# An S4 convolution beside a gated linear unit: the first normalisation moved to ScalarE, lag 2048 brought in by accumulating DMAs, the last tile split 384 and 128, and a new order

## The chip, the cores and the metric

The kernel runs on 1 core of one Trainium2 chip. The metric is the device time of one execution in microseconds (us), the median of several runs. The core has five engines, and each works through its own queue of instructions in order: TensorE (PE in the profile; its weight loads are PEld), VectorE (DVE), ScalarE (ACT), GpSimd (POOL) and SyncE (SP), which here issues nearly all DMAs.

## The reference

A layer normalisation without weights feeds two branches, whose outputs are added to the input. L = 2048 tokens, D = 512 channels, N = 128 modes a channel, F = 1792; inputs and output are bf16.

```python
x  = A_u                                   # (1, 2048, 512)
xn = (x - mean(x)) / sqrt(var(x) + 1e-5)   # over the 512 channels

# branch A: a long convolution in every channel
dt = exp(log_dt)
K  = real(sum_n C[d,n] * exp(dt*A[d,n])**l * dt*B[d,n])   # (512, 2048)
y  = irfft(rfft(pad(xn.T, 2L)) * rfft(pad(K, 2L)))[:, :L] # cast to bf16
yA = y.T + xn * Dskip

# branch B: a gated linear unit
h  = sigmoid(xn @ w_gate) * (xn @ w_up)    # (2048, 1792)
yB = h @ w_down

out = x + yA + yB
```

## The kernel before

**Start.** The 2048 tokens are 16 tiles of 128. Statistics are taken on VectorE (L542, L543; tile 2's on ScalarE instead, L533 to L538). From the variance comes 1/sqrt(var + eps): for the first four tiles VectorE adds epsilon (L486) and copies the mean (L489), POOL takes the square root as a power (L492), VectorE the reciprocal (L493); for the other groups of four tiles POOL adds epsilon (L481) and takes the power (L482). L554 normalises on VectorE. The first four tiles are transposed on TensorE (L565) and evicted into `xnT`, a pair of tiles at a time: the first pair whole by ScalarE (L572), the second whole by VectorE (L574). The others go through DRAM. While the inputs load, TensorE runs fillers (`keep_warm`, L519: 12, and then 3, 1 and 1).

**Branch B.** Four groups of 512 tokens, in each 14 tiles of F: gate (L1045), up (L1069), sigmoid on ScalarE (L1057), the product on VectorE (L1089, or L1094 straight from PSUM), then down (L1123). Its matmuls fill TensorE between those of branch A.

**Branch A.** The powers exp(dt A)^l are made as a table by squaring (L792 to L798) and complex products on VectorE (L737, L738, L742, L743). From the table TensorE makes pieces of K (L823). They are evicted to `kq_sb` (L288 on ScalarE, L286 on VectorE, by the list `ON_DVE`), stored to `k_scr` in DRAM and loaded again as `kT`, and L845 adds Dskip to lag 0. The convolution is a transform of xn (L695, then through `z_scr` in DRAM, L885), copies that swap halves (`f_sw`, L898), a transform of K (L911), the product of the two spectra on VectorE (L916, L920), an inverse transform in eight groups (L935), and a second step (S2, L994), for which the groups go through `v_scr` in DRAM.

**Lag 2048.** The transforms leave out one term for a few tokens. `f_rz` (L952) works out eight small values for each channel, L964 transposes them, ScalarE evicts them into `rr`, and S2 adds them with matmuls against a table `sr` (L997) in the tiles 12 to 15.

**End.** S2 of twelve tiles is added to branch B by VectorE, two tiles at once (L1020; the rows of x are already in `glu_sb`, put there by accumulating DMAs of POOL, L1160). In the last four tiles S2 is accumulated on top of the down projection in PSUM, and VectorE adds the rows `xt` of x (L1143). The very last tile is made in two halves of 256 columns.

**Order.** Every piece of work is an operation with a number, its place in the list `pl.ops`. A written list, `ORDER`, gives the order in which they are issued to the engines' queues; nothing is decided at run time but waits on semaphores. `ON_DVE` holds the numbers of the evictions and normalisations that go to VectorE rather than ScalarE. The results of matmuls stand in PSUM, in two pairs of 128x1024 f32 (`pair_63`, `pair_64`) and four banks of 128x512 f32.

## Time and profile before

| What | Value |
| --- | --- |
| Runs, median of 3 | 213.82 us (213.72, 213.82, 217.08) |
| Span of the profiled execution | 213.6 us |
| Own time of the profiled execution | not given; its span is 0.2 us below the median of the runs |
| TensorE busy | 204.2 us (96%), 1838 matmuls |
| VectorE busy | 191.3 us (90%), 406 instructions |
| ScalarE busy | 177.1 us (83%), 284 |
| POOL busy | 27.8 us (13%), 32 |
| Moved by DMA | 42.61 MB, 199 GB/s over the span |

Busy time is the sum over the engine's instructions. The span runs from the first to the last instruction of the profiled execution, and times in it are counted from its start. The granted clock of TensorE is at full speed in all of the 40 slices of the page.

### The profile page before, as it was taken

The numbers are of one execution on the slowest core, as the hardware profiler recorded it, in microseconds if no ns is written. First come the engines' busy times: TensorE is split into PE (matmuls) and PEld (weight loads), VectorE is DVE, ScalarE is ACT, GpSimd is POOL, SyncE is SP. The second block draws the span as 40 slices with busy tenths as digits, with TensorE's granted clock in tenths as the row PEclk, the third lists the DMA queues.
The fourth block names the chain that finished last, engine by engine and source line by source line (L and its number), as shares of the span: only waits on it lengthen the run. The fifth ranks groups of instructions, "written<-read, shape, count | busy, mean of one in ns | idle before, by whom it ended". The sixth has DMA issues, their size and how long they took to land.

```text
span 213.6 us, 4875 instructions
## 1 busy us (share of the span) xinstructions
PE 204.2 (96%) x1838; PEld 102.9 (48%) x1864; DVE 191.3 (90%) x406; ACT 177.1 (83%) x284; POOL 27.8 (13%) x32
## 2 busy tenths in 40 slices
...
GB/s 148 316 383 381 100 147 324 61 98 147 110 126 104 76 105 229 213 191 151 249 185 141 228 202 237 215 221 175 202 188 208 217 284 274 141 357 218 240 213 172
DMA packets 52377, 42.61 MB, mean 199 GB/s; under 512 B 16641, under 2 KB 44546, under 8 KB 52354
## 3 DMA queue, kind: packets, MB, share of 16 engines
...
q10 hardware_dynamic: 832, 0.43, 0.8%
q8 instruction: 14, 0.23, 0.5%
...
## 4 chain that ended last, share of the span: by engine, by line
PE 41%; DVE 40%; POOL 6%; DMA 4%; issue 4%; ACT 3%; DVEq 0%; SPq 0%; ACTq 0%
PE pair L911 8%; PE bank L1045 7%; PE bank L1123 7%; PE bank L1069 7%; DVE big L737 6%; DVE big L738 6%; POOL ln_ve_b L481 5%; PE pair L935 5%; DVE big L742 4%; DVE big L743 4%; DVE stats L542 3%; DVE hT_sb L1094 3%; DVE hT_sb L1089 3%; DVE big L678 2%; DMA big<-v_scr 2%
## 5 line engine op out<-in xcount | busy, mean ns | idle before, releaser
L288 ACT ACTIVATE big<-pair 128x1024 bf16<-128x1024 f32 x64 | 64.5, 1039 | 6.9 <-DVE big L920 1.7
L1069 PE MATMUL bank<-xnT,wu_sb 128*128 128x512 bf16 x214 | 52.9, 379 | 1.7 <-issue 0.6
L1123 PE MATMUL bank<-wd_sb,hT_sb 128*128 128x512 bf16 (+1 forms) x231 | 50.6, 367 | 0.5 <-issue 0.2
L1045 PE MATMUL bank<-xnT,wg_sb 128*128 128x512 bf16 (+1 forms) x191 | 45.6, 370 | 1.0 <-issue 0.5
L1045 PEld LDWEIGHTS <-wg_sb 128*128 128x128 bf16 x240 | 22.5, 98 | 25.0 <-issue 3.2
L1123 PEld LDWEIGHTS <-hT_sb 128*128 128x128 bf16 x238 | 22.4, 98 | 24.9 <-issue 1.6
L1069 PEld LDWEIGHTS <-wu_sb 128*128 128x128 bf16 x224 | 20.7, 98 | 27.5 <-issue 5.4
L1057 ACT ACTIVATE hT_sb<-bank 128x512 bf16<-128x512 f32 x48 | 28.2, 627 | 0.7 <-PE bank L1045 0.7
L737 DVE TENSOR_TENSOR big<-big 128x1024 bf16<-128x1024 bf16 (+4 forms) x40 | 26.7, 667 | 0.2
L738 DVE TENSOR_TENSOR big<-big 128x1024 bf16<-128x1024 bf16 (+4 forms) x40 | 26.5, 663 | 0.0
L1084 ACT ACTIVATE us_sb<-bank 128x512 bf16<-128x512 f32 x40 | 23.6, 616 | 0.6 <-DVE hT_sb L1089 0.3
L911 PE MATMUL pair<-big 128*128 128x256 bf16 x160 | 19.8, 273 | 0.0
L916 DVE TENSOR_TENSOR big<-big 128x2048 bf16<-128x2048 bf16 x16 | 19.3, 1217 | 0.1
L911 PEld LDWEIGHTS <-big 128*128 128x128 bf16 x160 | 15.4, 98 | 4.7 <-issue 0.8
L481 POOL TENSOR_SCALAR ln_ve_b<-mvb 128x4 bf16<-128x4 bf16 x3 | 13.0, 4323 | 34.1 <-DVE mvb L543 34.1
L742 DVE TENSOR_TENSOR big<-big 128x512 bf16<-128x512 bf16 (+4 forms) x40 | 16.5, 413 | 0.2
L743 DVE TENSOR_TENSOR big<-big 128x512 bf16<-128x512 bf16 (+4 forms) x40 | 16.5, 412 | 0.0
L792 ACT ACTIVATE sq_sb<-big 128x256 bf16<-128x256 bf16 (+2 forms) x20 | 13.2, 658 | 1.6 <-DVE big L743 1.5
L1089 DVE TENSOR_TENSOR hT_sb<-hT_sb,us_sb 128x1024 bf16<-128x1024 bf16 x20 | 13.5, 683 | 0.0
L935 PE MATMUL pair<-big 64*64 64x512 bf16 (+1 forms) x256 | 13.1, 327 | 0.0
L898 DVE COPY big<-big 32x1024 bf16<-32x1024 bf16 x20 | 8.4, 418 | 4.5 <-ACT big L288 4.2
L288 ACT ACTIVATE big<-big 128x256 bf16<-128x256 bf16 x30 | 12.4, 452 | 0.0
...
## 6 DMA issues: line engine op xcount, KB each, us to landing
...
z_scr<-big SPq DMA_DIRECT2D x16, 256.0 KB, 2.9
big<-z_scr SPq DMA_DIRECT2D x16, 256.0 KB, 4.2
v_scr<-big SPq DMA_DIRECT2D x16, 256.0 KB, 3.2
...
```

Of the source, the lines that this page charges most:

```text
L288: nc.scalar.activation(out=get(out), in_=get(in_), func=ACT.Identity)
L481: P.tensor_scalar(out=q["ve_b"], in0=mvb[:, s, 1], scalar1=EPS, scalar2=None, op0=ALU.add)
L737: V.tensor_tensor(out=wide(outp), in0=wide(lo), in1=mre, op=ALU.mult)
L738: V.tensor_tensor(out=wide(tb()), in0=wide(lo), in1=mim, op=ALU.mult)
L742: V.tensor_tensor(out=outp[:, :, 0], in0=outp[:, :, 0], in1=tb()[:, :, 1], op=opr)
L743: V.tensor_tensor(out=outp[:, :, 1], in0=outp[:, :, 1], in1=tb()[:, :, 0], op=opi)
L911: T.matmul(two(sk)[:, o:o + DW], es()[:, g, kt, :], kTv[p][:, :, kt, :], start=kt in (0, NKT - 1), stop=kt >= NKT - 2)
L935: T.matmul(two(sv)[o:o + 64, DW * (2 * g + y):2 * DW * (g + 1)], mab[b:b + 64, 2 * u + g, q, :], pq()[b:b + 64, q, ch] if y else pp()[b:b ...
L1045: T.matmul(bank(sl, k % 2)[:, c0:c1], w[:, kt, k * 128:(k + 1) * 128], xnT[:, grp, kt, c0:c1], start=(kt == 0), stop=(kt == KT - 1))
L1057: S.activation(out=hT_sb[:, hs.idx, k % 2, :], in_=bank(sl), func=ACT.Sigmoid)
L1069: T.matmul(bank(sl), wu_sb[:, kt, k * 128:(k + 1) * 128], xnT[:, grp, kt, :], start=(kt == 0), stop=(kt == KT - 1))
L1123: T.matmul(bank(po)[:, 0:c[1] - c[0]], hT_sb[:, hts[k // 2].idx, k % 2, jj * 128:(jj + 1) * 128], wd_sb[:, k, c[0]:c[1]], start=first and ...
```

## The change

1. The first four tiles: the statistics go to `mv` in f32, and the power is replaced by two ScalarE instructions, a logarithm and an exponential, exp(-0.5 ln(var + eps)), with an explicit load of the ScalarE function table that holds both. Tile 2's statistics return to VectorE. In the other groups epsilon is added on ScalarE instead of POOL.
2. The evictions of the transposed first tiles are halved: four of 128x512, three on VectorE and one on ScalarE. The gate matmuls that use halves wait for these.
3. The fillers on TensorE: 9 ahead, and 3 after the first transposes.
4. Lag 2048: one transposing matmul with 32 rows, one eviction, one store to DRAM (`r_scr`), and two accumulating POOL DMAs that add the rows to `xt`. The table `sr`, the clearing of `rr` and the five matmuls L997 are gone.
5. The last tile is made in 384 and 128 columns. The 384 columns take S2 after the down projection, the 128 ahead of it, as both halves did before.
6. `ORDER` is new, and `ON_DVE` holds five operations more: an eviction of the first transform (128x1024), two small casts in the making of K's seeds (128x256), one eviction of `kq_sb` (128x768) and one of the second transform (128x2x2x256).

The core of the diff (the table `ORDER`, of 927 numbers before and 923 after, is left out):

```diff
-ON_DVE = (86, 89, 104, 106, 121, 122, 123, 137, 138, 184, 194, 195, 198, 199, 201,)
+ON_DVE = (81, 84, 99, 101, 116, 117, 118, 132, 133, 154, 179, 189, 192, 194, 226, 242, 289, 335, 361, 516,)
...
-    rz = const.tile([128, KT, 8], BF, name="rz")
+    rz = const.tile([128, 8, KT], BF, name="rz")
+    rr = const.tile([8 * KT, 128], BF, name="rr")
...
         if t1 <= LN_ACT:
-            o_v = pl.add("DVE", 0.17 + 0.53 * len(set(range(t0, t1)) & set(ON_ACT)), fv_, deps, prio)
-            o_w = pl.add("DVE", 0.14, fw_, [o_v], prio)
-            o_p = pl.add("POOL", 0.7, lambda: P.tensor_tensor(out=q["sd_b"], in0=q["ve_b"], in1=half[:, s], op=ALU.pow), [o_v], prio)
-            return pl.add("DVE", 0.15, lambda: V.reciprocal(out=q["ri_f"], in_=q["sd_b"]), [o_p, o_w], prio)
+            def fr_():
+                S.activation(out=lnv[:, s], in_=mv[:, s, 1], func=ACT.Ln, bias=epst[:])
+                S.activation(out=q["ri_f"], in_=lnv[:, s], func=ACT.Exp, scale=-0.5)
+            return pl.add("ACT", 0.45, fr_, deps, prio)
 
         def fm_():
+            S.activation(out=q["ve_b"], in_=mvb[:, s, 1], func=ACT.Identity, bias=epst[:])
             S.activation(out=q["m_f"], in_=mvb[:, s, 0], func=ACT.Identity)
...
+    S.add_instruction(mybir.InstLoadActFuncSet(name=nc.get_next_instruction_name(), act_func_set_id=LN_EXP_SET))
...
-    keep_warm(12, -10)
-    for n in (0, 5, 6):
-        keep_warm(3 if n < 3 else 1, -9 + n)
+    warm = [keep_warm(9, -10)]
...
+            tr = pl.add("PE", 0.80, ft, [xn_ready[i - 1], xn_ready[i], l_id] + warm[-1:], prio, acq=[sl])
+            if i == 1:
+                warm.append(keep_warm(3, prio, [tr]))
+            half_ready.append([])
+            for n, eng in enumerate(("DVE", "DVE" if i == 1 else "ACT")):
+                def fe(i=i, sl=sl, n=n, eng=eng):
+                    ks = slice(2 * n, 2 * n + 2)
+                    dst, src = xnT[:, 0, ks, (i - 1) * 128:(i + 1) * 128], bankb(sl).rearrange("p (k n) -> p k n", k=KT)[:, ks]
...
-    o_rt = pl.add("PE", 0.32, f_rt, [o_rz], 60, acq=[slr])
-    o_rz = pl.add("ACT", 0.48, lambda slr=slr: S.activation(out=rr[0:8, :], in_=bank(slr)[0:8, :], func=ACT.Identity), [o_rt, l_sr, m_rr], 60, rel=[slr])
+    o_rt = pl.add("PE", 0.08, lambda slr=slr: T.matmul(bank(slr)[0:8 * KT, 0:128], rz[:].rearrange("p q k -> p (q k)"), ident[:], start=True, stop=True),
+                  [o_rz], 60, acq=[slr])
+    o_rr = pl.add("ACT", 0.25, lambda slr=slr: S.activation(out=rr[:], in_=bank(slr)[0:8 * KT, 0:128], func=ACT.Identity), [o_rt], 60, rel=[slr])
+    r_st = dma("SP", r_scr[:], rr[:], deps=[o_rr], prio=60, pkt=256)(8 * KB)
...
-        if i >= 12:
-            T.matmul(o[64:128, :], sr[:, i - 12, :], rr[:, w[0]:w[1]], start=False, tile_position=(0, 64), **kw)
...
+                    def fc(n, xt=xt):
+                        with nc.allow_non_contiguous_dma(reason="laid out"):
+                            P.dma_start(out=xt[95:128:32, n::2, :], in_=r_v[n], accum_op=ALU.add)
+                    lx = [pl.add("POOL", 1.0, lambda n=n: fc(n), lx + [r_st], 3, dma=(4 * KB, _rate(256), 1.0)) for n in range(2)]
...
-            cols = [(0, 256), (256, 512)] if last else [(0, 512)]
-            ver = vp_op[i // 2] + [l_s2, o_rz]
+            cols = [(0, 384), (384, 512)] if last else [(0, 512)]
+            ver = vp_op[i // 2] + [l_s2]
```

What the new order does shows in the engines' queues. A row names a line and an operation, what it writes and reads and the shape; x2 stands for two in a row. Lines count in the kernel before and in the changed kernel: L565 becomes L548, L1045 L1031, L695 L684, L743 L732, L823 L812, L845 L834, L898 L885, L916 and L920 L903 and L907, L935 L922, L994 L981, L1020 L1006, L1094 L1080, L1123 L1115, L1143 L1136, L286 and L288 L285 and L287.

**VectorE at the start of the program**, before; `xnT` does not appear, since its first eviction is ScalarE's:

```order
L542 BN_STATS stats<-big 128x6 x2
L543 BN_AGGR mvb<-stats 128x2 x2
L486 TENSOR_SCALAR ln_ve_b<-mvb 128x2
L489 CAST ln_m_f<-mvb 128x2
L542 BN_STATS stats<-big 128x6
L543 BN_AGGR mvb<-stats 128x2
L493 RECIPROCAL ln_ri_f<-ln_sd_b 128x2
L554 TENSOR_SCALAR big<-big,ln_m_f,ln_ri_f 128x512 x2
L486 TENSOR_SCALAR ln_ve_b<-mvb 128x2
L489 CAST ln_m_f<-mvb 128x2
L493 RECIPROCAL ln_ri_f<-ln_sd_b 128x2
L554 TENSOR_SCALAR big<-big,ln_m_f,ln_ri_f 128x512 x2
```

And the same place now, behind the first two tiles' statistics (L599, L607 and L608 belong to the products with dt, and 128x2x256 are half evictions):

```order
L525 BN_STATS stats<-big 128x6
L526 BN_AGGR mv<-stats 128x2
L537 TENSOR_SCALAR big<-big,mv,ln_ri_f 128x512 x2
L525 BN_STATS stats<-big 128x6
L526 BN_AGGR mv<-stats 128x2
L562 COPY xnT<-pair_63 128x2x256
L537 TENSOR_SCALAR big<-big,mv,ln_ri_f 128x512 x2
L599 TENSOR_TENSOR big<-big 128x512 x2
L562 COPY xnT<-pair_64 128x2x256
L562 COPY xnT<-pair_63 128x2x256
L607 TENSOR_SCALAR big<-big 128x512
```

The third tile's statistics now stand ahead of the first normalisation, the small steps for epsilon, mean and reciprocal are gone, and the second half of the first pair (`pair_63`) comes behind the second pair's normalisation, two products with dt and the second pair's first half.

**VectorE at the second Dskip addition** (`dskr`), just behind the last complex products, before:

```order
L920 TENSOR_TENSOR big<-big 128x1024 x2
L898 COPY big<-big 32x1024 x4
L845 TENSOR_TENSOR big<-big,dskr 1x16x16
L898 COPY big<-big 32x1024 x4
L1094 TENSOR_TENSOR hT_sb<-hT_sb,bank_68 128x512
L916 TENSOR_TENSOR big<-big 128x2048
```

And now (the casts L285 are the evictions of `kq_sb` and of the second transform that were ScalarE's):

```order
L285 CAST kq_sb<-pair_63 128x96x8
L903 TENSOR_TENSOR big<-big 128x2048
L907 TENSOR_TENSOR big<-big 128x1024 x2
L1080 TENSOR_TENSOR hT_sb<-hT_sb,bank_67 128x512
L285 CAST big<-pair_64 128x2x2x256
L1080 TENSOR_TENSOR hT_sb<-hT_sb,bank_65 128x512
L834 TENSOR_TENSOR big<-big,dskr 1x16x16
L1080 TENSOR_TENSOR hT_sb<-hT_sb,bank_66 128x512
L885 COPY big<-big 32x1024 x8
L903 TENSOR_TENSOR big<-big 128x2048
```

The addition of Dskip stood behind four of the swapping copies; now it stands ahead of all eight, with three products of branch B and two evictions around it.

**SyncE near the end**, now, where the last groups of the inverse transform are stored and loaded again (`v_scr`) and the first output leaves:

```order
L422 DMA v_scr_103<-big 128x4x256 x2
L422 DMA xnT<-v_scr_102 128x2x1024
L422 DMA v_scr_104<-big 128x4x256
L422 DMA big<-v_scr_103 96x2x1024
L422 DMA r_scr<-rr 32x128
L422 DMA big<-v_scr_104 32x2x1024
L422 DMA big<-v_scr_103 96x2x1024 x2
L422 DMA big<-v_scr_104 32x2x1024
L422 DMA out_dram<-big 128x1024
L422 DMA big<-v_scr_103 96x2x1024
```

Before, two stores `v_scr_101` stood side by side here and both led to the reloads; now there is one, the store of the lag rows `r_scr` stands among the reloads, and one reload of `v_scr_103` has moved behind the first output.

97 lines of the change are left out of this document (39 added, 58 removed), and 81 rows, old and new, of the table ORDER.

## The prediction

> **What bounds the kernel now.** I read the page first: its span, the engines' shares (first section) and the shares of the chain that ended last (fourth section). Then, by windows, two stages of 20 us: their ends, then length, then busy time of PE, PEld, DVE and ACT.
>
> ```profile
> span 213.6 us, 4875 instructions
> PE 204.2 (96%) x1838; PEld 102.9 (48%) x1864; DVE 191.3 (90%) x406; ACT 177.1 (83%) x284; POOL 27.8 (13%) x32
> ...
> PE 41%; DVE 40%; POOL 6%; DMA 4%; issue 4%; ACT 3%; DVEq 0%; SPq 0%; ACTq 0%
> ...
> 120.00:140.00 20.00, 19.79 (x273) 10.60 (x275) 19.97 (x47) 19.02 (x30) 0.00 (x0) 1.00 0.76 211
> ...
> 160.00:180.00 20.00, 19.48 (x193) 10.95 (x192) 15.60 (x28) 18.50 (x24) 0.00 (x0) 1.00 0.83 240
> ```
>
> TensorE and VectorE share the chain almost evenly, and from 120 to 140 both are full; VectorE has room in 160 to 180 (15.60 of 20). So work taken from TensorE counts only if VectorE keeps up. The timeline (start, length, engine, line, operation, how many; in brackets the wait ahead and who ended it) shows that the program falls into pieces at three points: the last product that makes K (C, L823), the last inverse product (V, L935), and the first matmul of the last transform (S2, L994).
>
> ```profile
> 154.65 0.43 DVE L743 TENSOR_TENSOR big<-big 128x512 bf16<-128x512 bf16 x1
> ...
> 155.04 1.51 PE L823 MATMUL pair<-big 128*32 128x82 bf16 x128
> ...
> 163.95 1.71 DVE L898 COPY big<-big 32x1024 bf16<-32x1024 bf16 x4 [4.20 <-ACT big L288]
> 165.69 0.28 DVE L845 TENSOR_TENSOR big<-big,dskr 1x256 bf16<-1x256 bf16 x1
> ...
> 166.05 2.35 PE L911 MATMUL pair<-big 128*128 128x256 bf16 x20
> ...
> 188.06 1.28 DVE L920 TENSOR_TENSOR big<-big 128x1024 bf16<-128x1024 bf16 x2
> 188.35 1.51 PE L935 MATMUL pair<-big 64*64 64x512 bf16 x32
> ```
>
> C begins when VectorE ends its last complex product (L743) and ends at 156.55. From there to the end of V at 189.86 is 33.3 us. VectorE waits 4.20 us once and then has no idle time to 189.34. The chain in order of time goes on from there (start, length, who), and after it the timeline of VectorE:
>
> ```profile
> 190.22 1.03 ACT big L288
> 191.27 2.59 DMA v_scr<-big
> 193.92 4.70 DMA big<-v_scr
> 198.67 0.95 PE pair L994 x14
> ...
> 203.34 1.94 DVE L1143 TENSOR_TENSOR big<-bank,big 128x512 bf16<-128x512 f32 x3 [1.76 <-PE bank L997]
> ...
> 210.06 0.41 DVE L1143 TENSOR_TENSOR big<-bank,big 128x256 bf16<-128x256 f32 x1
> ```
>
> From V to S2 the way is an eviction, a store and a reload: 198.67 - 189.86 = 8.8 us. The last 10 us are VectorE's: from 203.34 to 210.47 its additions stand end to end, 14.9 us from S2 to the end of the span.
>
> The three runs are 213.72, 213.82 and 217.08; the span is 213.6, and no time of its own is given for the profiled execution. I add the terms to the span and then 0.2 for the way to the median.
>
> **Term 1, up to C.** The start first, from the timeline, and the group of ScalarE's smallest steps (busy, mean ns).
>
> ```profile
> 1.43 5.30 PE L519 MATMUL bank<-glu_sb 128*128 128x512 bf16 x12 [1.43 <-POOL rz L513]
> 7.10 1.24 PE L519 MATMUL bank<-glu_sb 128*128 128x512 bf16 x5
> 8.48 0.44 PEld L1045 LDWEIGHTS <-wg_sb 128*128 128x128 bf16 x4 [0.64 <-DMA wg_sb<-in_B_w_gate_dram]
> 8.61 0.60 PE L1045 MATMUL bank<-xnT,wg_sb 128*128 128x256 bf16 x4 [0.26 <-ACT xnT L572]
> 11.57 0.60 PE L1045 MATMUL pair<-xnT,wg_sb 128*128 128x256 bf16 x4 [0.61 <-DVE xnT L574]
> 5.74 0.73 DVE L554 TENSOR_SCALAR big<-big,ln_m_f,ln_ri_f 128x512 bf16<-128x512 bf16 x2
> ...
> L536 ACT ACTIVATE stats<-mv 128x1 f32<-128x1 f32 x1 | 0.2, 187 | 0.0
> ```
>
> With the power on POOL the first normalisation starts at 5.74. With two small ScalarE instructions (0.19 us each by L536, taken as 0.45 with their waits) it could start at 5.0, but the order puts a third tile's statistics ahead, so 5.35. Then the halved evictions: the first pair's second half now stands behind two more normalisations and the two products with dt. VectorE's queue gives 6.95 + 0.4 (copy) + 0.75 (normalise) + 1.3 (products, which wait for the exponential) + two copies of 0.35, so that half is in place at 10.05. Before, TensorE began at 8.61, worked 1.74 us on halves (16 x 0.109) and waited to 11.57: as good as an unbroken start at 9.83. Now it is about 9.9, and it could not have been ahead of the weights at 8.48. **The start gains nothing**, between -0.6 and +0.5.
>
> VectorE's work up to C does change. The rows are its groups (count, busy, mean ns, idle before), and the last one from the table of waits (total, count, longest).
>
> ```profile
> L1020 DVE TENSOR_TENSOR big<-pair,glu_sb 128x1024 bf16<-128x1024 f32 x4 | 4.7, 1216 | 6.5 <-PE pair L994 6.5
> L574 DVE COPY xnT<-pair 128x1024 bf16<-128x1024 bf16 x1 | 0.7, 684 | 0.0
> L286 DVE COPY big<-big 128x256 bf16<-128x256 bf16 x6 | 1.7, 282 | 0.0
> L542 DVE BATCH_NORM_STATS2 stats<-big 128x6 f32<-128x512 bf16 x15 | 9.8, 680 | 2.9 <-DMA big<-in_A_u_dram 2.9
> L543 DVE BATCH_NORM_AGGREGATE mvb<-stats 128x2 bf16<-128x6 f32 x15 | 2.3, 169 | 0.0
> L661 DVE CAST big<-big 128x512 bf16<-128x512 f32 x4 | 1.5, 424 | 0.0
> ...
> DVE ln_ri_f L501 <- POOL ln_sd_b L482: 1.2, 1, 1.2
> ```
>
> Added: one eviction of 128x1024 from PSUM, not shown on VectorE as a copy; by L574 0.7, by L1020 1.2. I take 1.2, as L1020 too reads f32 from PSUM. Two seed copies, 2 x 0.28; tile 2's statistics, 0.65 + 0.16; three half evictions at 0.35 for one of 0.68. Removed: L486, L489 and L493 twice each, about 0.15 a piece (L543, of a like size, takes 0.17). Net 1.2 + 0.56 + 0.81 + 0.37 - 0.9 = 2.0. In return the 1.2 us wait for POOL goes, since the addition of epsilon leaves POOL. C comes **0.8 later**; 0 if the eviction takes 0.7 and one copy hides in a wait, 2.0 if the pow is as late as the addition was.
>
> The Trainium skill, "VectorE: DVE Perf Modes", section "Why PSUM operands drop a tier", says that an f32 operand in PSUM is held to one element a cycle; by it the eviction costs the 1.2 taken here. L661 (f32 in SBUF, 512 in 0.42 us) would make it 0.8 and C 0.4 earlier, if PSUM did not matter.
>
> TensorE's own work up to C falls: one group of 0.86 more stands behind C (17 instead of 15 groups of four up to V, 4 instead of 8 matmuls just behind V), and two changes of tile shape go. Its reserve ahead of C is about 1 us, so VectorE decides.
>
> **Term 2, C to V.** The order shows the Dskip addition (L845, now L834) and what stands behind it. It waits for K's way through DRAM. The rows are the last evictions of K (timeline), the last store and the reload (DMA issues, each with its time to landing), and two groups of VectorE.
>
> ```profile
> 155.97 1.51 ACT L288 ACTIVATE kq_sb<-pair 128x768 bf16<-128x768 f32 x2 [0.23 <-PE pair L823]
> ...
> DMA to landing us min/median/max: 2.9/2.9/2.9
> ...
> DMA to landing us min/median/max: 3.7/3.7/3.7
> ...
> L916 DVE TENSOR_TENSOR big<-big 128x2048 bf16<-128x2048 bf16 x16 | 19.3, 1217 | 0.1
> L898 DVE COPY big<-big 32x1024 bf16<-32x1024 bf16 x20 | 8.4, 418 | 4.5 <-ACT big L288 4.2
> ```
>
> That makes C + 1.0 + 2.9 + 3.7 = C + 7.6, with the SyncE queue and the addition C + 8.0. Before, the addition ended at C + 9.4, because four copies (1.71) stood ahead of it. Now all eight copies and L1080 stand behind it. From it to the last L907 VectorE has 8 pairs of L903/L907 (1.14 + 0.60 from start to start; the 1.22 of the row overlaps its neighbour), 20 copies (0.43), four products (0.6) and the five rz instructions (0.5): 25.4, with the 0.8 of gaps that the same stretch shows before, 26.2; so V's input at C + 34.1 instead of C + 32.8. **+1.3.** If the reload lands later (4.8 us is the longest beside it) +2.5; if TensorE alone decided, its matmuls from C to V come to 31.4 us and 20 changes of tile shape, C + 33.8 at about 0.12 each (an estimate from gaps in the records), which is +0.5. The two evictions put into the 4.20 us gap (kq and one of x) cost nothing: they stand where VectorE waits anyhow.
>
> **Term 3, V to S2.** Only one V group is last now, so one eviction, not two, precedes the store: 0.2 + 1.05 + 2.6 + 4.7 = 8.55; one reload of 384 KB has moved behind the first output, which I take for another 0.25. **-0.5** (-0.9 to -0.1). TensorE's cover is 7.2 us (0.86 + 6.2 and two switches), so it waits about 1 us; that is not added, the DMAs decide.
>
> **Term 4, S2 to the end.** The five lag matmuls (L997) leave, and VectorE's block can start 0.2 earlier. Its sum stays: 384 + 128 columns for 256 + 256. The last transfer is now 256 KB behind L1006, where 64 KB stood beside it before; by the row of the page's DMA issues it lands in 2.1. **-0.1** (-0.4 to +0.2).
>
> ```profile
> out_dram<-big SPq DMA_DIRECT2D x7, 256.0 KB, 2.1
> ```
>
> Sum: 213.6 + 0.8 + 1.3 - 0.5 - 0.1 = 215.1, and 215.3 for the median. That is no change within the 2% that a measurement of this kernel can tell.
>
> **Rivals.** *TensorE stays the bound* (faster). If VectorE's additions fit into waits, C comes at 156.55 - 0.86 - 0.2 = 155.5, V 33.8 later, S2 8.3 after that, the end 14.8 after that: 212.4. With the median's 0.2, 212.6. For it: TensorE has the larger share, and its shape changes fall from 78 stretches to 70. Against it: VectorE's 19.97 of 20. Range 211.6 to 213.8.
>
> *The array starts cold* (slower). The first row of the start shows 12 filler matmuls in 5.30 us, 0.43 us each; the second 5 in 1.24, 0.25 each: full speed came only after about 5.1 us of unbroken stream. Nine last 3.8 us, then TensorE waits about 0.5 us for the first normalised tile. If the unbroken stream is what counts, it starts anew at 10, and 5.1 us at half speed are 2.5 us of matmuls late. TensorE's reserve takes up to half of that: 1.3 to 2.5 on 215.3, so 217.4. It decides from the point where the gap breaks the count.
>
> The Trainium skill, "TensorE: Matmul & The Clock Gate", section "Part 1: The HAM clock gate", says that the array needs one busy window of about 3.4 us, and that the windows run freely; by it 3.8 us rarely hold a whole window, and the price is half of 3.4 to 6.8 us, an estimate of 1.7 to 3.4. The trace agrees in that 5.1 us were needed.
>
> *The accumulating DMAs come late.* The lag row now goes to DRAM and is added to xt by two POOL DMAs, for which the additions at S2 + 4.45 wait.
>
> ```profile
> c_scr<-k_scr SPq DMA_DIRECT2D x2, 1.0 KB, 3.4
> ...
> DMA to landing us min/median/max: 4.3/5.3/7.4
> ```
>
> The store is issued at V + 1.7 and lands in 3.4 by the first row; two issues of about 1 us; the accumulating DMAs of the second row (256 KB) land in 4.3 to 7.4: V + 11.4 to 14.4, against V + 12.8 wanted. At worst 1.6 late, all of it on VectorE's last block: 216.9. Small ones should land sooner, so I give it little.
>
> **How the numbers follow.** Forecast 215.3 (213.8 to 216.8): 0.50. TensorE bound 212.6: 0.29. Cold start 217.4: 0.11. Late DMAs 216.9: 0.10. The range takes most of the second case and up to the worst terms: 212.0 to 217.3. Faster by over 2% (below 209.5) needs both engines to gain: 0.03. Slower by over 2% (above 218.1), a cold start on top of late terms: 0.05. Within: 0.92.
>
> **What would show it.** Term 1: the last L732 ends near 155.9 instead of 155.1, and C waits for it. Term 2: VectorE idle ahead of L834, none from there to the last L907. Term 3: TensorE idle about 1 us ahead of L981. The cold start: filler and first gate matmuls 0.43 us apart beyond 10 us. Late DMAs: L1136 waiting for a DMA. Wrong altogether if C comes earlier than 155: then VectorE had reserves that I did not see.

## The result and the profile after

| | Runs | Median, us | Ratio to before, 95% interval |
| --- | --- | --- | --- |
| before, in the same comparison | 4 | 214.35 (213.72 to 217.08) | |
| changed | 4 | 222.64 (221.19 to 222.97) | 1.036 (1.029 to 1.042) |
| changed, again on another chip, before there 215.03 | 4 | 220.60 (219.27 to 222.61) | 1.025 (1.020 to 1.029) |

Now and then an execution, of any version, runs some per cent slower at a lower clock; ratios leave such runs out, and a row marked * has its stretches from one. The change makes the kernel slower, by 2.5 to 3.6%. The forecast was 215.3 (212.0 to 217.3) with no change. The lines of the changed kernel's page that answer to those of before (span, engines, shares of the chain that ended last):

```profile
span 221.2 us, 4841 instructions
PE 203.3 (92%) x1827; PEld 101.9 (46%) x1853; DVE 195.2 (88%) x409; ACT 172.1 (78%) x279; POOL 16.2 (7%) x29
PE 29%; ACT 23%; DMA 20%; DVE 17%; issue 4%; SPq 4%; POOL 1%; DVEq 0%; ACTq 0%
```

TensorE has as much work as before, but in a longer span, and DMAs hold 20% of the chain where they held 4%. The chain in order of time shows where (start, length, who); behind it the two waits in the timelines of VectorE and TensorE:

```profile
159.74 5.84 DMA k_scr<-kq_sb
...
165.63 2.76 DMA big<-k_scr
...
168.41 0.29 DVE big L834
...
168.75 3.42 PE pair L898 x20
```

```profile
168.41 0.28 DVE L834 TENSOR_TENSOR big<-big,dskr 1x256 bf16<-1x256 bf16 x1 [3.54 <-DMA big<-k_scr]
...
168.75 3.42 PE L898 MATMUL pair<-big 128*128 128x256 bf16 x20 [2.86 <-DVE big L834]
```

K's way through DRAM is now the chain: VectorE waits 3.54 us for it and TensorE 2.86, where before TensorE's L911 had no wait at all. The twenty matmuls behind it last 3.42 us instead of 2.35. By windows of the changed kernel (length, PE, PEld, DVE, ACT and POOL busy, then granted clock, DMA share, GB/s) the clock halves about a microsecond after the gap:

```profile
166.00:168.00 2.00, 0.00 (x0) 0.00 (x0) 0.00 (x0) 0.69 (x1) 0.00 (x0) 1.00 0.50 135
168.00:170.00 2.00, 1.25 (x11) 1.12 (x12) 1.55 (x4) 0.00 (x0) 0.00 (x0) 0.96 0.76 222
170.00:172.00 2.00, 2.00 (x12) 1.40 (x10) 1.93 (x6) 1.02 (x1) 0.00 (x0) 0.50 0.84 181
172.00:174.00 2.00, 2.00 (x8) 0.82 (x7) 1.48 (x3) 1.34 (x2) 0.00 (x0) 0.68 0.79 198
174.00:176.00 2.00, 2.00 (x19) 0.51 (x17) 2.00 (x3) 1.87 (x4) 0.00 (x0) 1.00 0.76 245
```

Four points cut every profile into stretches: **kq**, the start of ScalarE's evictions of K's last product; **Ds**, the start of the Dskip addition that waits for K (L834); **V**, the end of the last inverse product; **S2**, the first matmul of the last transform behind its wait. The forecast's terms, put in the same form (kq is 0.6 ahead of C, Ds is C + 7.7), stand beside what was measured:

| Profiled execution | to kq | kq to Ds | Ds to V | V to S2 | S2 to end | span |
| --- | --- | --- | --- | --- | --- | --- |
| before | 156.0 | 9.7 | 24.2 | 8.8 | 14.9 | 213.6 |
| forecast | 156.8 | 8.3 | 26.9 | 8.3 | 14.8 | 215.1 |
| changed | 157.9 | 10.5 | 29.1 | 8.9 | 14.8 | 221.2 |
| changed, again | 157.8 | 10.3 | 27.7 | 8.1 | 15.2 | 219.1 |

Of the 6.1 us that the forecast lacks, 1.1 lie ahead of K, 2.2 on K's way, 2.2 between K and V, and 0.6 behind; of the 4.0 in the repeat it is 1.0, 2.0, 0.8 and 0.2. Why K's way is longer is seen in SyncE's queue (start, length of the issue). Changed kernel first, with POOL's accumulating DMA of the same time, and then the kernel before:

```profile
156.64 0.37 SPq L422 DMA_DIRECT2D v_scr<-big  x1
157.05 0.51 SPq L422 DMA_DIRECT2D big<-k_scr  x1
...
158.22 0.58 SPq L422 DMA_DIRECT2D v_scr<-big  x1
159.72 0.58 SPq L422 DMA_DIRECT2D k_scr<-kq_sb  x1
...
165.63 0.36 SPq L422 DMA_DIRECT2D big<-k_scr  x1
...
157.40 0.88 POOL L1153 DMA_DIRECT2D big<-in_A_u_dram  x1 [12.82 <-ACT big L287]
```

```profile
154.74 0.53 SPq L422 DMA_DIRECT2D big<-c_S  x1
157.51 0.58 SPq L422 DMA_DIRECT2D k_scr<-kq_sb  x1
...
160.88 0.52 SPq L422 DMA_DIRECT2D big<-k_scr  x1
```

Before, SyncE issued nothing in the 2.2 us ahead of K's store, and from its issue to that of the reload, which waits for it, it took 3.4 us. Now two stores of `v_scr` (256 KB each), an earlier reload of `k_scr` and 256 KB from POOL go out just ahead, and it takes 5.9 (5.4 in the repeat).

### The profile page after: what moved, and what is told of

It reads as the page before. It is cut to its first block, busy times and chain, and to the rows that moved or that the text cites. A ratio compares the mean times of both kernels' runs of the same rounds, so it can differ in the third digit from the quotient of the medians.

```text
span 221.2 us, 4841 instructions
## 1 busy us (share of the span) xinstructions
PE 203.3 (92%) x1827; PEld 101.9 (46%) x1853; DVE 195.2 (88%) x409; ACT 172.1 (78%) x279; POOL 16.2 (7%) x29
## 4 chain that ended last, share of the span: by engine, by line
PE 29%; ACT 23%; DMA 20%; DVE 17%; issue 4%; SPq 4%; POOL 1%; DVEq 0%; ACTq 0%
PE pair L898 7%; PE bank L1055 7%; DMA big<-z_scr 6%; PE bank L1115 5%; ACT big L658 4%; ACT big L652 4%; PE bank L1031 4%; SPq L422 4%; ACT hT_sb L1043 3%; DVE big L726 3%; DVE big L727 3%; PE pair L922 3%; DMA k_scr<-kq_sb 3%; ACT big L287 3%; DMA big<-c_E 3%
## 5 line engine op out<-in xcount | busy, mean ns | idle before, releaser
L287 ACT ACTIVATE big<-pair 128x1024 bf16<-128x1024 f32 x62 | 63.1, 1045 | 14.7 <-PE pair L898 8.1
L1055 PE MATMUL bank<-xnT,wu_sb 128*128 128x512 bf16 x214 | 53.3, 380 | 0.8 <-issue 0.2
L1115 PE MATMUL bank<-wd_sb,hT_sb 128*128 128x512 bf16 (+2 forms) x233 | 50.0, 367 | 0.2
L1031 PE MATMUL bank<-xnT,wg_sb 128*128 128x512 bf16 (+1 forms) x189 | 46.2, 374 | 1.7 <-DVE xnT L562 1.0
L1031 PEld LDWEIGHTS <-wg_sb 128*128 128x128 bf16 x240 | 22.8, 99 | 25.5 <-issue 4.0
L1115 PEld LDWEIGHTS <-hT_sb 128*128 128x128 bf16 x238 | 22.0, 98 | 25.6 <-issue 1.8
L1055 PEld LDWEIGHTS <-wu_sb 128*128 128x128 bf16 x224 | 20.7, 98 | 25.5 <-issue 3.4
L1043 ACT ACTIVATE hT_sb<-bank 128x512 bf16<-128x512 f32 x48 | 29.2, 643 | 0.5 <-PE bank L1031 0.4
L1070 ACT ACTIVATE us_sb<-bank 128x512 bf16<-128x512 f32 x40 | 25.1, 643 | 1.3 <-PE bank L1055 0.8
L898 PE MATMUL pair<-big 128*128 128x256 bf16 x160 | 20.4, 282 | 3.1 <-DVE big L834 2.9
L903 DVE TENSOR_TENSOR big<-big 128x2048 bf16<-128x2048 bf16 x16 | 19.5, 1219 | 0.9 <-ACT big L287 0.5
L898 PEld LDWEIGHTS <-big 128*128 128x128 bf16 x160 | 15.9, 101 | 8.2 <-DVE big L834 3.4
L732 DVE TENSOR_TENSOR big<-big 128x512 bf16<-128x512 bf16 (+4 forms) x40 | 16.6, 414 | 0.0
L525 DVE BATCH_NORM_STATS2 stats<-big 128x6 f32<-128x512 bf16 x16 | 10.6, 680 | 3.0 <-DMA big<-in_A_u_dram 3.0
L658 ACT ACTIVATE big<-big 128x1024 f32<-128x1024 f32 x11 | 12.8, 1161 | 0.0
L922 PE MATMUL pair<-big 64*64 64x512 bf16 (+1 forms) x256 | 12.7, 327 | 0.0
L652 ACT ACTIVATE big<-big 128x512 bf16<-128x512 f32 x20 | 12.2, 727 | 0.0
```

Source lines behind the costliest of these rows:

```text
L287: nc.scalar.activation(out=get(out), in_=get(in_), func=ACT.Identity)
L652: S.activation(out=W[p][:, k], in_=cur[:, :, DW * p:DW * p + DW], func=ACT.Identity)
L658: s_op = pl.add("ACT", 0.95, lambda cur=cur, sq=sq: S.activation(out=sq, in_=cur, func=ACT.Square), [cur_op] + W_op[-1:], PLAD + k * 0.01)
L898: T.matmul(two(sk)[:, o:o + DW], es()[:, g, kt, :], kTv[p][:, :, kt, :], start=kt in (0, NKT - 1), stop=kt >= NKT - 2)
L903: V.tensor_tensor(out=pp().rearrange("p q h m -> p (q h) m"), in0=xx().rearrange("p q h m -> p (q h) m"), in1=kb()[:, 0:2 * DW].unsqueeze( ...
L1031: T.matmul(bank(sl, k % 2)[:, c0:c1], w[:, kt, k * 128:(k + 1) * 128], xnT[:, grp, kt, c0:c1], start=(kt == 0), stop=(kt == KT - 1))
```

## The experiments

The theories, in words. **Store:** the transfers ahead of K's store make it late. **Gap:** TensorE runs dry at K's wait and its clock falls, which costs more than the wait. **Start:** parts 1 to 3 make K itself late, through ScalarE. **Behind:** the order has put more work behind the wait for K than TensorE and VectorE can do in the old time. The expectations put these in their own words. Every experiment has its own runs of the kernel before on the same chip. Numbers in a diff are pieces of `ORDER`; "..." leaves out the rest. Lines of the experiments' kernels can differ by one to four from the changed kernel's.

**First comparison, four repairs of K's wait** (before there 214.96). In the first, the two stores of `v_scr` (487, 412) go behind K's store:

```diff
-..., 515, 884, 487, 843, ..., 505, 878, 412, 441, 516, 362, 550, ..., 426, 364, 365, ...
+..., 515, 884, 843, ..., 505, 878, 441, 516, 362, 487, 550, ..., 426, 364, 412, 365, ...
```

> The changed kernel, with two 256 KB stores to v_scr on SyncE moved: one behind the last store of K to k_scr (issued at 159.7 us, it lands after 5.84 us), the other behind the reload of K. Theory Q (the store of K lands late because those stores stand ahead of it on the DMA engines): it lands in about 3 us, L834 starts near 166 instead of 168.4, TensorE's wait of 2.86 us ahead of L898 falls below 0.6, its clock does not fall after it, and the time comes down by 3 to 4.5 us to about 218. Theory P (what it competes with is the accumulating DMA of 256 KB that POOL issues at 157.4): the store still takes 5 us or more and the time stays within 0.7 of the changed kernel's. Theory F (too little work of TensorE behind C, whatever the store does): TensorE still waits over 1.5 us, gain below 1.5.

In the second, POOL's accumulating DMA (810) goes behind K, by a small POOL copy (923) that reads `kT`:

```diff
+    pl.add('POOL', 0.1, lambda: P.tensor_copy(out=late_w[32:33, :], in_=kT[1][32:33, 7, 0, 0, 0:2]), (k_ld[-1],), 0)
-..., 426, 364, 365, ..., 856, 561, 810, 549, ...
+..., 426, 364, 923, 810, 365, ..., 856, 561, 549, ...
```

> The changed kernel, with a tiny POOL copy that reads the reloaded K put ahead of the last accumulating DMA into glu (256 KB, issued at 157.40 us, landing after 5.1), so that this DMA starts only when K is back. Theory P: the store of K lands in about 3 us instead of 5.84, L834 at about 166, TensorE's wait of 2.86 goes, 3 to 4.5 us gained. Theory Q: the store still takes over 5 us, the time stays within 0.7. Both can have a share: then each of the two runs gains 1 to 2.5.

In the third, two groups of gate matmuls (with what belongs to them, 882 to 895) go ahead of the transform of K; in the fourth, twelve idle matmuls fill the gap:

```diff
-..., 426, 364, 365, 569, 490, 507, 882, 886, 570, 508, 887, 506, 895, 868, ...
+..., 426, 364, 882, 886, 887, 868, 895, 365, 569, 490, 507, 570, 508, 506, ...
```

> The changed kernel, with two gate groups of TensorE (2 x 0.86 us), their sigmoids and one product that stand behind the first L898 moved ahead of the second Dskip addition in the order, so that TensorE has seven groups between the last piece of K and L898, as before the change, instead of five. Theory F (the wait of 2.86 us is missing cover, K's way being as long as it is): the wait falls to about 1.1 us, the clock stays up or falls for less, 1.7 to 3 us gained. If the wait itself is the cost that counts and the work is only moved ahead of VectorE's limit: gain below 0.7, and VectorE has no idle time from L834 on.

```diff
+    def warm_fn():
+        for _ in range(12):
+            T.matmul(bank(warm_sl), wg_sb[:, 0, 0:128], wd_sb[:, 0, :], start=True, stop=True)
-..., 364, 365, 569, ...
+..., 364, 365, 923, 569, ...
```

> The changed kernel, with twelve filler matmuls of 128x512 (12 x 0.216 = 2.6 us) ahead of the first L898 behind the wait for K: the wait stays, TensorE is only kept busy in it. Theory H (the idle 2.86 us let the clock fall, and the 20 matmuls L898 behind it take 3.42 us instead of 2.36): L898 takes 2.4, the granted clock is 1.0 from 168 to 180 instead of 0.84, 1 to 1.6 us gained. If the slow L898 came from anything else, or VectorE sets the pace there: no gain, within 0.5, or 0.3 to 0.6 lost where the fillers end late.

| | Median, us | Ratio (95%) | to kq | kq to Ds | Ds to V | V to S2 | S2 to end |
| --- | --- | --- | --- | --- | --- | --- | --- |
| stores behind | 220.63 | 1.026 (1.018 to 1.034) | 156.6 | 8.7 | 27.9 | 8.9 | 14.8 |
| POOL behind | 220.30 | 1.024 (1.020 to 1.028) | 157.2 | 8.2 | 29.6 | 8.9 | 14.8 |
| more fill | 221.04 | 1.028 (1.024 to 1.032) | 157.7 | 9.3 | 28.3 | 8.8 | 15.3 |
| gap filled | 220.56 | 1.026 (1.021 to 1.030) | 157.2 | 10.0 | 27.8 | 9.2 | 14.8 |

Store is right about K's way: each half of the repair takes 1.6 to 2.3 us off it. But none of the four brings the loss back: beside the changed kernel's first runs (1.036) each is about 1% better, beside its repeat (1.025) none is. In the second repair what was won ahead of Ds is lost again by V. TensorE waits there for the constants `c_E` of the transform, whose load was issued 1.1 us earlier than in the repeat (176.55 for 177.60), with Ds 2.8 earlier (timeline of TensorE, POOL behind):

```profile
165.67 2.36 PE L898 MATMUL pair<-big 128*128 128x256 bf16 x20 [0.92 <-DVE big L834]
...
183.38 0.83 PE L898 MATMUL pair<-big 128*128 128x256 bf16 x6 [2.26 <-DMA big<-c_E]
```

The wait for `c_E` is 0.27 and 0.55 in the changed kernel and 1.71 with more fill; the kernel before has none. No run took it away, so what it costs is not shown. And Gap is not the bound: with the gap full of matmuls, useful or not, the stretch behind it is not below 27.8, where the repeat has 27.7.

**Second comparison, the parts and the order taken apart** (before 215.03). The first kernel has parts 1 to 5 with the old order and the old `ON_DVE`; the second has the new order with the old parts; the third has the eight swapping copies (490, 491 and 517) ahead of the Dskip addition again; the fourth is the changed kernel once more.

```diff
-ON_DVE = (..., 132, 133, 154, 179, 189, 192, 194, 226, 242, 289, 335, 361, 516,)
+ON_DVE = (..., 132, 133, 179, 189, 190, 193, 194, 196,)
-ORDER: that of the changed kernel
+ORDER: that of before, with the numbers of the changed kernel
```

> The changed kernel's parts 1 to 5 (logarithm and exponential, halved evictions, fillers, lag 2048 by accumulating DMAs, 384 and 128 columns) in the order of the kernel before, and with its list ON_DVE; only the operations that the parts add or remove are fitted in. Theory O (the new order is what costs): within 1% of the kernel before, 212.5 to 216 where that takes 214 to 215; K is back before 166 and from the second Dskip addition to the last inverse product it takes 24 to 25 us, as before. Theory S (single parts cost: the store and two DMAs of lag 2048, or the last tile): 218 or more.

```diff
 parts 1 to 5: as before
-ORDER, ON_DVE: those of before
+ORDER, ON_DVE: those of the changed kernel, with the numbers of before
```

> The kernel before with the new order and the new ON_DVE alone, none of the parts 1 to 5 (operations that it has and the changed kernel has not stand at the nearest place). Theory O: 219 to 223 us, with the stretch from the second Dskip addition to the last inverse product at 27 us or more. Theory S: within 1% of the kernel before.

```diff
-..., 426, 364, 365, 569, 490, 507, ..., 580, 517, 552, ..., 566, 491, 893, ...
+..., 426, 364, 517, 490, 491, 365, 569, 507, ..., 580, 552, ..., 566, 893, ...
```

> The changed kernel, with the first eight swapping copies (L885, 3.4 us of VectorE) and the ScalarE eviction that half of them wait for moved ahead of the second Dskip addition, into VectorE's wait of 3.5 us. Theory V (from L834 on VectorE sets the pace, 25.4 us of work against 24.2 in the whole stretch before): 2 to 3.4 us gained, the stretch from L834 to the last inverse product falls from 29.1 to 26 or less. Theory T (TensorE and the loads of c_E set the pace there): below 0.8 gained, VectorE waits for ScalarE's evictions or TensorE in the middle of the stretch instead.

> The changed kernel once more, on the chip of the three others, as their reference: 221 to 223 us, 1.03 to 1.04 of the kernel before. All theories say the same of it. What it tells is how far the milestones move from one execution to the next: the last product of K was at 158.6, K's store took 5.84 us.

| | Median, us | Ratio (95%) | to kq | kq to Ds | Ds to V | V to S2 | S2 to end |
| --- | --- | --- | --- | --- | --- | --- | --- |
| parts, old order | 219.86 | 1.026 (1.019 to 1.033) | 158.6 | 11.5 | 24.2 | 8.6 | 14.9 |
| order alone * | 226.15 | none | 159.7 | 10.6 | 28.6 | 8.8 | 15.7 |
| copies ahead | 222.25 | 1.034 (1.030 to 1.038) | 156.9 | 10.5 | 28.9 | 7.7 | 16.1 |
| changed again | 220.60 | 1.025 (1.020 to 1.029) | 157.8 | 10.3 | 27.7 | 8.1 | 15.2 |

The order alone scattered from 221.75 to 228.21, so it has no ratio; its lowest run is still 3% above before. The parts in the old order lose as much as the whole change, but elsewhere: behind Ds they are as fast as before, and all of it lies ahead (11.5 from kq to Ds, with a pause of 1.7 that the third comparison shows). So two losses, each about as large as the whole, do not add up. The third kernel shows that the copies were not in the way: ahead of the addition they only uncover the wait behind it, since VectorE's next product (L903) needs the transform of K and its eviction.

The changed kernel's second profile sets the clock apart from the rest, since here TensorE's gap was shorter and the clock held (timeline and window of the repeat):

```profile
168.45 2.36 PE L898 MATMUL pair<-big 128*128 128x256 bf16 x20 [2.32 <-DVE big L834]
...
160.00:180.00 20.00, 17.68 (x169) 9.22 (x165) 16.23 (x29) 14.85 (x18) 0.00 (x0) 1.00 0.80 217
```

From Ds (168.11) to the end of the last L907 (194.39) it took 26.3 us, with VectorE full; in the first profile, with the clock at half for some 3 us and VectorE waiting 0.51 and 0.94 for ScalarE, 27.7.

**Third comparison, the start and the split** (before 214.95). The first kernel has parts 4 and 5 alone in the old kernel (`f_rz`, `r_scr`, the two accumulating DMAs, the last tile in 384 and 128 columns). The second is parts 1 to 5 in the old order, but with one whole eviction for each of the first pairs:

```diff
-            for n, eng in enumerate(("DVE", "DVE" if i == 1 else "ACT")):
+            for n, eng in enumerate(("ACT" if i == 1 else "DVE",) * 2):
...
-                    ks = slice(2 * n, 2 * n + 2)
+                    if n:
+                        return
+                    ks = slice(0, KT)
```

> The kernel before with parts 4 and 5 alone (lag 2048 by a store and two accumulating DMAs, last tile in 384 and 128 columns), everything else and the order as before. Where parts 1 to 5 in the old order ended 4 us late, the loss stood ahead of the last piece of K (160.3 us against 156.0), and from there to the end the times were those of before. Theory N (the tail parts are neutral, the start parts cost): within 0.5 us of the kernel before. Theory L (the accumulating DMAs come late): VectorE waits ahead of its last additions, 1 us or more slower. Theory G: five matmuls, a load and a clearing less give 0.5 us or more.

> As the run of parts 1 to 5 in the old order, but the evictions of the first transposes whole again: the first pair by ScalarE, the second by VectorE, as before the change. Theory A (in that run ScalarE stood 1.9 us before its half eviction, which waited for VectorE, so that the chain of ScalarE up to the first sigmoid came 1.6 us later, and ScalarE is the full engine from 10 to 60 us): the first sigmoid comes at 15.3 to 15.8 instead of 16.9, and 1.3 to 2 us come back. Theory B (the addition of epsilon on ScalarE, for which VectorE waited 2.1 us at 23.4, costs most): below 0.8 back. The rest of the 4 us is then the other theory's.

The third is the kernel before with two groups of four branch-B matmuls moved from ahead of K's transform to behind it; the fourth is the changed kernel with three of the repairs at once (stores behind, more fill, copies ahead).

```diff
-..., 522, 449, 860, 559, 883, 560, ..., 573, 514, 572, 884, 515, ..., 592, 593, 853, ...
+..., 522, 449, 559, 560, ..., 573, 514, 860, 883, 572, 515, ..., 592, 593, 884, 853, ...
```

> The kernel before, with two groups of up matmuls (2 x 0.86 us) moved from ahead of the first L911 behind the second Dskip addition to behind the second L911: nothing is added, TensorE has five groups instead of seven between the last piece of K and the wait for K. Theory W (the work that stands ahead of a wait is what counts; behind it all that is left stands end to end): TensorE waits 1.5 us or more ahead of L911 and the time grows by 1.4 to 2.2 us, or by more if the clock falls in the wait. Theory V (VectorE sets the pace from the addition on, TensorE has room): below 0.5.

> The changed kernel with three repairs of its order around the last piece of K: the two stores to v_scr behind K's store, two gate groups of TensorE with what belongs to them ahead of the Dskip addition, and eight swapping copies with their eviction ahead of it too. Theory W: K is back near 165.3, TensorE does not wait for it over 0.5 us, the stretch from the Dskip addition to the last inverse product takes 26 to 27 us instead of 28 to 29, in all 216 to 218, still 1 to 2% slower than the kernel before since ten groups stand behind the addition where eight did. If the loads of c_E set the pace in that stretch, it stays at 28 us and the time at 218.5 or more.

| | Median, us | Ratio (95%) | to kq | kq to Ds | Ds to V | V to S2 | S2 to end |
| --- | --- | --- | --- | --- | --- | --- | --- |
| parts 4 and 5 alone | 215.66 | 1.003 (1.000 to 1.006) | 154.8 | 9.7 | 24.2 | 8.8 | 14.8 |
| whole evictions, old order | 218.51 | 1.016 (1.011 to 1.021) | 156.7 | 11.5 | 24.2 | 8.4 | 15.6 |
| before, two groups behind K | 217.40 | 1.012 (1.007 to 1.016) | 156.0 | 9.7 | 25.8 | 8.4 | 14.9 |
| changed, three repairs * | 221.97 | 1.030 (1.025 to 1.035) | 157.2 | 11.0 | 29.9 | 7.8 | 16.9 |

The new lag and the new last tile cost nothing and bring nothing. So parts 1 to 3 are what loses 2.3% in the old order, and halving the evictions is about 1% of that (1.026 against 1.016, on two chips, with intervals that just overlap). In the old order the place is ScalarE. Its timeline in the parts with the old order:

```profile
10.71 0.60 ACT L560 ACTIVATE xnT<-pair 128x512 bf16<-128x512 bf16 x1 [1.88 <-DVE xnT L562]
...
16.92 1.09 ACT L1043 ACTIVATE hT_sb<-bank 128x512 bf16<-128x512 f32 x2
```

The half eviction waits 1.88 us for VectorE's half, everything of ScalarE stands behind it, and the first sigmoid comes at 16.92; before, the whole eviction stood at 7.55 and the first sigmoid at 15.36. That is not caught up, since ScalarE before has nothing to spare there (its windows of 10 us, the fourth busy time):

```profile
10.00:20.00 10.00, 9.34 (x55) 5.29 (x55) 9.86 (x21) 9.85 (x15) 1.90 (x2) 1.00 1.06 379
...
40.00:50.00 10.00, 9.95 (x53) 4.34 (x52) 10.00 (x32) 10.00 (x17) 1.36 (x1) 1.00 0.16 54
50.00:60.00 10.00, 9.95 (x53) 4.36 (x53) 9.63 (x17) 10.00 (x20) 9.92 (x2) 1.00 0.58 157
```

Whole evictions bring the first sigmoid to 15.01 and still lose 1.6%. What the profile shows beside it is VectorE's wait of 1.3 us for POOL's power, which now stands behind an addition on ScalarE (2.12 with the halves), and in both kernels a pause inside K's last product that no wait explains (timeline of TensorE, whole evictions):

```profile
155.74 1.43 PE L814 MATMUL pair<-big 128*32 128x82 bf16 x120
158.84 0.26 PE L814 MATMUL pair<-big 128*32 128x82 bf16 x8 [1.68 <-issue]
```

Against before, the halves are 1.6 us late at the first step of the table, 3.0 behind the wait for POOL's power and about 2.6 at kq; whole evictions are 0.4 early, then 1.1 and 0.7 late. The pause adds 1.7 to both. It stands in the changed kernel too, but is 0.21 there and 0.56 in the repeat.

In the changed kernel ScalarE's half eviction does not wait: it stands at 10.13, and the first sigmoid comes at 15.81, 0.45 behind before. So the two losses of the old order, the half eviction and the long pause, are not the changed kernel's.

The third kernel shows Behind on its own: nothing but two groups (1.7 us) moved across K's wait, TensorE waits 1.65 us ahead of L911, and it loses 1.2%. The fourth shows that the repairs do not add up.

**Fourth comparison, work taken away** (before 214.93). In the first kernel six groups behind K's wait do one matmul of four, in the second the same is done in the kernel before to six groups ahead of it:

```diff
+SHORT = (886, 895, 849, 847, 871, 851)
-                def fu(k=k, sl=b, grp=grp):
-                    for kt in range(KT):
+                def fu(k=k, sl=b, grp=grp, nk=1 if len(pl.ops) in SHORT else KT):
+                    for kt in range(nk):
```

> The changed kernel, in which six gate or up groups that stand between the first L898 behind the second Dskip addition and the last one make one of their four matmuls (18 of 128x512 left out, 18 x 0.216 = 3.9 us of TensorE; every other instruction stays). Theory W (behind the wait for K TensorE's work stands end to end and sets the end; the changed order has four groups more there): the last inverse product comes 3 to 4 us earlier, and 2.8 to 4 us are gained. Theory V (VectorE sets the pace there, 25.4 us of work): the stretch from the addition to the last inverse product stays above 27 us, below 1 gained.

> The kernel before, in which the six groups that stand last ahead of the wait for K make one of their four matmuls (the same 18 matmuls of 128x512 fewer, 3.9 us of TensorE). Theory W: nothing is gained, within 0.5 us, since TensorE only waits longer for K, 3 us or more; if the clock falls in that wait, 0.5 to 1.5 us slower, with less work. If work of TensorE counts wherever it stands: 2.5 to 4 us faster.

The third takes the old list, which gives the five operations back to ScalarE (in the diff eight entries go and three others come); the fourth has the first two repairs of K's wait together.

```diff
-ON_DVE = (..., 132, 133, 154, 179, 189, 192, 194, 226, 242, 289, 335, 361, 516,)
+ON_DVE = (..., 132, 133, 179, 189, 190, 193, 194, 196,)
```

> The changed kernel with the list ON_DVE of the kernel before: the evictions of the first transform, of K and of the second transform and the two more seed copies are ScalarE's again, in their places of the new order. Forecast's first term (VectorE is full up to the last product for K; the first eviction and the copies cost it 1.2 + 0.56): the last piece of K is ready 1.2 to 1.8 us earlier and 1 to 2 us are gained. Rival: ScalarE is the full engine from 10 to 60 us and the eviction there costs it as much; the last piece of K moves by less than 0.5, or later, and nothing is gained.

```diff
-..., 515, 884, 487, 843, ..., 505, 878, 412, 441, 516, 362, 550, ..., 426, 364, 365, ..., 561, 810, 549, ...
+..., 515, 884, 843, ..., 505, 878, 441, 516, 362, 487, 550, ..., 426, 364, 923, 810, 412, 365, ..., 561, 549, ...
```

> The changed kernel with the two stores to v_scr behind K's store and the accumulating DMA of POOL behind K's reload, both together. Theory Q+P (the three transfers share the DMA engines with K's store): it lands in 2.9 to 3.3 us, as before the change, instead of 5.84 (4.3 and 4.0 with one of them), L834 comes 7.5 to 8.0 us behind the first eviction of the last K instead of 10.5, TensorE waits below 0.5 us. In time 0.5 to 1.5 us better than either alone, 217 to 219: the groups behind remain. If the store still takes 4 us or more, something else slows it (the packets of 192 bytes themselves, the reload of the first half of K beside it).

| | Median, us | Ratio (95%) | to kq | kq to Ds | Ds to V | V to S2 | S2 to end |
| --- | --- | --- | --- | --- | --- | --- | --- |
| changed, 3.9 us less behind K | 220.11 | 1.024 (1.018 to 1.030) | 156.6 | 9.5 | 27.7 | 7.7 | 15.8 |
| before, 3.9 us less ahead of K | 215.17 | 1.003 (1.000 to 1.006) | 156.0 | 9.7 | 24.2 | 8.4 | 14.9 |
| casts on ScalarE | 223.66 | 1.043 (1.036 to 1.049) | 160.0 | 10.2 | 27.0 | 8.6 | 15.5 |
| stores and POOL behind | 219.03 | 1.020 (1.016 to 1.025) | 156.6 | 8.3 | 28.6 | 7.8 | 16.2 |

Taking 3.9 us of matmuls away behind K's wait leaves that stretch at 27.7, and VectorE took 26.5 us of it up to the last L907 as it did with them: TensorE's work does not set it, as far as one profile shows, in which its clock fell for some 4 us. Giving the casts back to ScalarE makes the kernel slower, with K 2.2 us later than in the repeat: VectorE has 1.1 us less to do up to the last complex product, but waits 9.0 instead of 6.0. With both repairs K's store is as fast as it was (SyncE's issues, stores and POOL behind):

```profile
158.03 0.57 SPq L423 DMA_DIRECT2D k_scr<-kq_sb  x1
...
161.54 0.52 SPq L423 DMA_DIRECT2D big<-k_scr  x1
```

That is 3.5 us against 5.9, and kq to Ds is the 8.3 of the forecast. The time falls by 0.4%, which is not certain (1.020 against 1.025, with intervals that overlap). In the profile V is 2.35 us earlier than in the repeat, and 1.0 of that is lost again behind S2: the additions L1137 begin 5.9 us behind S2, where the repeat needed 4.9 and the first profile 4.5. The wait's row names TensorE, but its matmuls had ended 0.8 us before, and the accumulating DMAs of the lag, issued by POOL at 200.39, took 6.4 and 6.7 us there; in the whole evictions the same wait names them (timeline of VectorE):

```profile
206.62 1.29 DVE L1138 TENSOR_TENSOR big<-bank,big 128x512 bf16<-128x512 f32 x2 [0.51 <-DMA big<-r_scr]
```

**Fifth comparison, both engines relieved** (before 215.02): less work behind K and the copies ahead, and then that with stores and POOL behind as well.

```diff
+SHORT = (886, 895, 849, 847, 871, 851)
-..., 426, 364, 365, 569, 490, 507, ..., 580, 517, 552, ..., 566, 491, 893, ...
+..., 426, 364, 517, 490, 491, 365, 569, 507, ..., 580, 552, ..., 566, 893, ...
```

> The changed kernel with both reliefs of the stretch behind the second Dskip addition: the eight copies and their eviction ahead of it (VectorE 3.4 us less behind it), and six groups behind it with one of their four matmuls (18 matmuls of 128x512 left out, TensorE 3.9 us less). Theory VT (TensorE and VectorE are both full there, 28.4 and 27.7 us with their waits, so that relief of one alone shows little): the stretch falls from 28 to 29 us to 24.5 to 26. If a third thing sets it (ScalarE's evictions, the loads of c_E): it stays at 27.5 or more.

```diff
 the same, and with it
-..., 884, 487, 843, ..., 878, 412, 441, 516, 362, 550, ..., 364, 517, 490, 491, 365, ..., 561, 810, 549, ...
+..., 884, 843, ..., 878, 441, 516, 362, 487, 550, ..., 364, 923, 810, 412, 517, 490, 491, 365, ..., 561, 549, ...
```

> As the run before in this pair (copies ahead, 18 matmuls left out), and K's store relieved too: the two v_scr stores and POOL's accumulating DMA behind it. Theory VT with a late K: the addition starts near 165, the stretch takes 24.5 to 26 us, the last inverse product ends at 189.5 to 191.5 where the kernel before has 189.9 and the changed kernel 195.8 to 197.5, and the time is within 1% of the kernel before. If much of the loss lies elsewhere, the last inverse product ends at 193 or later.

| | Median, us | Ratio (95%) | to kq | kq to Ds | Ds to V | V to S2 | S2 to end |
| --- | --- | --- | --- | --- | --- | --- | --- |
| both engines relieved | 221.18 | 1.027 (1.021 to 1.033) | 157.3 | 10.7 | 27.4 | 8.5 | 14.8 |
| all relieved | 220.94 | 1.025 (1.022 to 1.029) | 157.2 | 10.5 | 29.8 | 8.7 | 15.2 |

Neither gained. The first shows what bounds the stretch beside VectorE's sum (timeline of VectorE):

```profile
168.23 0.67 DVE L1081 TENSOR_TENSOR hT_sb<-hT_sb,bank 128x512 bf16<-128x512 bf16 x1
172.76 1.23 DVE L904 TENSOR_TENSOR big<-big 128x2048 bf16<-128x2048 bf16 x1 [3.86 <-ACT big L288]
```

With the copies gone from this place VectorE stands idle for 3.86 us, until K's transform is done and evicted; the copies had only filled that. In the kernel before the first product (L916) began 2.7 us behind Ds, here 4.7: it has to wait for the transform behind Ds, which took 3.31 instead of 2.35 as the clock fell again, and its eviction. Whether another order of the first two products would end that wait was not tried. No version is faster than the kernel before; parts 4 and 5 alone equal it.

## Why the prediction was wrong

**The bound.** Right that both engines were full and that VectorE sets the pace behind K: from Ds to the last L907 the forecast was 26.2 us and the repeat took 26.3. The rival in which TensorE stays the bound and the kernel gains (212.6, 0.29) is refuted: C did not come earlier.

**Term 1, +0.8 by the last L732 at 155.9.** It ended at 156.72 and 156.63 in the changed kernel's two profiles, and kq is 1.1 and 1.0 late against the forecast. That the start gains nothing was right. The eviction of 128x1024 had the forecast size (changed kernel, groups by shape: busy, mean ns, idle before), and so had VectorE's work as a whole (windows up to the end of the last complex product, before and then changed, columns as above):

```profile
L285 DVE CAST big<-pair 128x1024 bf16<-128x1024 f32 x2 | 2.5, 1226 | 0.5 <-ACT hT_sb L1043 0.5
...
0.00:155.08 155.08, 150.94 (x1240) 72.74 (x1259) 148.94 (x340) 144.27 (x243) 27.82 (x32) 1.00 0.67 189
...
0.00:156.72 156.72, 148.53 (x1230) 71.91 (x1248) 150.74 (x341) 139.95 (x238) 13.47 (x26) 1.00 0.64 184
```

VectorE is busy 1.8 us longer, and the forecast was 2.0. What did not come is the gain: VectorE is idle for 6.0 us as it was for 6.1, where the forecast took off the 1.2 us wait for POOL's power. That wait is still there, 0.9 long. But the size is small: over the twelve profiles with this start the complex product ends at 155.4 to 156.7, on average at 156.0, so term 1 held about as forecast. The way from there to the end of K's last product took 1.9 us instead of 1.5, partly by the pause (0.21).

**Term 2, +1.3 with the addition at C + 8.0.** This is the step that failed: 2.2 us on K's way and 2.2 behind it (2.0 and 0.8 in the repeat). "C + 1.0 + 2.9 + 3.7" took the store's landing from the kernel before, and from its page the longest reload as the bound; but what changed was what SyncE and POOL issue ahead of the store, and the store from its issue to the reload's grew from 3.4 to 5.9, and 5.4 in the repeat. The reload itself was quicker, 2.8. The copies had been moved behind the addition on the promise that it would be ready earlier; with it at kq + 10.5 instead of 8.3 the order has their cost and not its return. The store's part is shown, since moving just those transfers gave kq to Ds of 8.3 (0.2 to 0.6 of the difference is the pause in K's last product). It is not the whole: in that kernel Ds to V was 28.6, not 26.9, and the kernel still 2% slower than before.

**The cover that was not priced.** Term 2 counted TensorE as one sum from C to V. It has to be split at the wait: of its gate and up groups there the old order had seven ahead of K's transform and eight behind, the new one five and twelve. So TensorE ran dry for 2.3 to 2.9 us, and in the first profile the clock fell, where Ds to V was 29.1 instead of 27.7. Moving two groups behind in the old kernel costs 1.2%, so the mechanism is real; yet filling the gap in the changed kernel brought nothing against the repeat, which fits VectorE's 26.2 us starting at Ds in any case. The last step, from the last L907 to V, is 1.4 instead of 0.5, as two groups of four (L1055, 1.9 us) stand between the last inverse products.

**Terms 3 and 4, -0.5 and -0.1.** Measured +0.1 and -0.1 in the first profile, -0.7 and +0.3 in the repeat. In all profiles without a * V to the end is 23.2 to 24.1 us, before 23.7: where S2 comes sooner, the additions come later. TensorE's wait ahead of L981, forecast at about 1, was 1.36 (timeline of TensorE, changed kernel).

```profile
204.72 0.30 PE L981 MATMUL pair<-xnT,big 128*64 128x256 bf16 x2
206.38 0.30 PE L981 MATMUL pair<-big 128*64 128x256 bf16 x2 [1.36 <-DMA big<-v_scr]
```

**Late DMAs (0.10).** Not in the changed kernel, where L1136 waits for TensorE. But the rival is the next bound: with S2 earlier it takes 1.0 to 1.4 us back, which is read from one profile and named by the trace in another, and was not isolated.

**Cold start (0.11).** It comes in some executions and not in others, and no price is seen. In the first profile the nine and three fillers were followed by gate matmuls at full speed (timeline of TensorE, first the changed kernel, then its repeat).

```profile
6.19 0.62 PE L548 MATMUL pair<-ident,big 128*128 128x128 bf16 x8 [0.71 <-DVE big L537]
6.64 0.81 PE L514 MATMUL bank<-glu_sb 128*128 128x512 bf16 x3
...
10.86 1.04 PE L1031 MATMUL pair<-xnT,wg_sb 128*128 128x256 bf16 x8
...
6.59 1.03 PE L548 MATMUL pair<-ident,big 128*128 128x128 bf16 x8 [1.11 <-DVE big L537]
7.42 1.49 PE L514 MATMUL bank<-glu_sb 128*128 128x512 bf16 x3
...
10.67 0.81 PE L1031 MATMUL bank<-xnT,wg_sb 128*128 128x256 bf16 x6 [0.59 <-DVE xnT L562]
```

In the first profile the last three fillers take 0.81 us together, where the first nine took 4.02, and the gate matmuls are at full speed behind a gap of 0.71. In the repeat, behind a gap of 1.11, the transposes and the three fillers are slow again, and the gate matmuls are fast only from 10.67; yet kq is 157.8 there and 157.9 in the first profile.

**What stays open.** K's slow store is shown to be the work of the transfers ahead of it, and with them out of the way 2% remain (219.03). Of that the profile names VectorE's 26 us behind Ds with the wait for K's transform in them, the waits for `c_E` and the late additions behind S2; no run has removed them one by one to the old time. Parts 1 to 3 with whole evictions lose 1.6% in the old order, most of it in the pause of 1.7 us, whose cause the runs do not show.
